# Indicator rows by engine copies, norm weights loaded later, the last row tile in two banks, and half of the first norm rows turned by DMA

## The chip, the cores and the metric

The kernel runs on one core of one Trainium2 chip. The metric is the time of one execution on the device in microseconds (us); lower is better. A core has five engines, each with an instruction stream of its own that it runs in order: TensorE (PE in the profile), VectorE (DVE), ScalarE (ACT), GpSimd (POOL) and SyncE (SP). Weight loads of TensorE have a row of their own (PEld). Engines wait for each other, and for transfers, on semaphores. Transfers are issued from the queues of SP, ACT and POOL; here SP issues nearly all of them, POOL those that change the type on the way (v and the weights).

## The reference

Attention in which each query may look at six chunks of 32 keys, and then a gated feed-forward network (FFN) on the normed result.

```python
# q, k, v: (4, 8, 768, 64)
k_min, k_max = np.min(k_chunks, axis=3), np.max(k_chunks, axis=3)     # 24 chunks of 32 keys
ub = np.sum(np.maximum(q * k_min, q * k_max), axis=-1)                # bound of each chunk
ub = np.where(causal, ub, -1e9)
top_chunks = np.argsort(ub, axis=-1)[..., -6:]
scores = np.matmul(q, k.transpose(0, 1, 3, 2)) / 8
scores = np.where(sel & (pos[:, None] >= pos[None, :]), scores, -1e9)
attn = softmax(scores) @ v
# x: (3072, 512), the attention with its heads side by side
xn = x / np.sqrt(np.mean(x * x, axis=-1, keepdims=True) + 1e-6) * rms_g
g = xn @ w_gate                                                       # 512 -> 1536
out = (g * sigmoid(g) * (xn @ w_val)) @ w_out                         # 1536 -> 512
```

## The kernel before

**A planner writes the order.** The kernel is first built as a list of steps: `add(name, engines, duration, rank, emit, dependencies, opens=..., uses=...)`. `Order.run` then plays the list through with rough durations of its own. Whenever an engine is free it takes, of the steps whose dependencies are done and for whose buffers there is room, the one with the lowest rank; where a step may run on several engines the first free one has it. The instructions are written out in the order in which the steps started. Ranks are sums of constants: `RANK` by kind of step, `TIMES` by place (`a3`: preparation of pair 3, `l3` its loads, `s3.0` its scores, `n0.1` and `f0.1` norm and FFN of batch 0, second half). So a change of one constant can move instructions on all engines. On the chip nothing of that play-through is left but the order: each engine runs its own stream and waits where its operands aren't there yet.

**Attention.** The 32 heads come as 16 pairs (4 per batch). For each pair `prep` loads k and q, turns them on TensorE in threes into PSUM (`pk`, `pq`, L525), evicts them (`kt`, `qt`, L297 on ACT or L301 on DVE), reduces each chunk of 32 keys to its minimum and maximum on DVE (`ku` L556, `kmx` L554, one instruction each for 768 columns) and takes their difference (`dif`, L607, on DVE or POOL). The bounds matmuls (`ub`, L731 for one pair, L789 for two together from pair 6 on) need these and the queries. The bounds are turned back (`up`), masked, and for each query the six best chunks are found on DVE (`MAX8`, L658) and written as a selection (`sel`, L673 to L687), which is turned into rows of the query operand `QS`.

**The indicator rows.** The score matmul (`sc`, L876) contracts over 128 rows: 64 of the head and, beside them, rows that say in `KE` to which chunk a key belongs and in `QS` which chunks a query has chosen; unchosen keys get a large negative score. The rows of `KE` are the same for all pairs: `e_all`, made once on POOL, stands in all three sets of buffers (`SLOTS["set"]` is 3, two heads each). In the kernel before set 0 gets them by two copies on ACT or DVE (`ke0`), sets 1 and 2 by four DMAs on the SP queue (`ke`, L393 and L394).

**Scores to rows.** `exp` on ACT (L893, `pt`), the causal mask on POOL, the product with v on TensorE (`av`, L912), and a division on DVE into `xb`, the rows of a batch.

**Norm and FFN.** `norm` takes three row tiles (half a batch): sums of squares, a root on POOL (`ri`, L981), then on DVE `xs`, the row times its root and the norm weights `gains` (L989). `xs` is turned to `xT`: in batch 0 by four TensorE transposes a row tile (`tp`, L1011) and an eviction, in the other batches by one transposing DMA on SP (L1000). `ffn` then does for 12 blocks of the 1536 columns a `gate` block (4 matmuls, L1045), `tanh` on ACT (`sg`, L1052), `tg` on DVE (L1058), a `val` block (4 matmuls, L1066) and `hh` on DVE (L1074); and for three row tiles 12 matmuls into one PSUM bank (`po`, L1086), an eviction (`osb`, L297 to L303) and a store.

**Fillers.** `busy` (L346) multiplies zeros by zeros: 48 matmuls of 512 columns and 40 of 256 with a rank so high that the planner takes one only where it has nothing else for TensorE. Once written they stand in TensorE's stream and run, whatever the chip's timing.

Of the kernel before, what the change touches and what calls it, by code (L numbers as in the profile page):

```python
# [8 lines left out]
FP32 = mybir.dt.float32  # L9
# [15 lines left out]

RANK = (
    dict(
        av=439.71, dif=-349.0, eps=-276.35, exp=56.9, kC=119.11, kE=221.89, kT=-479.5,
        kload=-91.99, kmn=-561.73, kmx=-221.73, max=-117.69, qC=120.39, qE=644.67, qN=97.14,
        qT=303.27, qX=110.23, qload=17.43, relu=-156.64, root=392.56, sc=392.96, sel=176.91,  # L30
        selC=388.0, selT=-168.59, sq=-325.5, tp=-47.15, tpE=460.17, ub=-387.44, ubE=-1000.64,
        ubm=-238.37, up=-379.03, vload=-360.06, xb=-167.37, xs=293.02,
    ),
    dict(
        av=-243.01, dif=-122.81, eps=-968.41, exp=80.0, gate=-57.45, hh=-33.27, kC=474.21,
        kE=54.78, kT=-28.02, kload=327.35, kmn=571.37, kmx=673.95, mask=-6.85, max=351.72,
        out=-338.93, po=268.25, poE=188.61, qE=-4.14, qN=444.8, qT=271.57, qX=-691.62,
        qload=314.07, relu=202.91, root=-1348.37, sc=-186.72, sel=354.08, sq=285.76, tanh=579.3,
        tg=-259.04, ub=-101.04, ubE=-390.25, ubm=307.49, up=-117.99, val=-52.48, vload=103.56,
        xT=119.23, xb=-299.83, xs=-84.52,  # L40
    ),
)

TIMES = {
# [15 lines left out]
}  # L60


# [139 lines left out]
def kernel(  # L202
# [51 lines left out]
    def add(name, engs, occ, rank, *a, **kw):  # L254
        return order.add(name, engs, occ, rank if isinstance(rank, dict) else {"": rank}, *a, **kw)
# [126 lines left out]
    for n in range(4):  # L382
        prev = add("e_all", "POOL", 0.82, -80 + n, lambda e, n=n: e_step(n), [prev])
    c_e = prev
    c_ke = [None] * NB
    for i in range(NB):
        if i == 0:
            c_ke[i] = add("ke0", "", {"DVE": 1.05, "ACT": 1.4}, {"ke0": 1.0}, lambda e: (
                evict(e, KE[0][0][D:2 * D, :], e_all[:]),
                evict(e, KE[0][1][0:D, :], e_all[:])), [c_e])  # L390
        else:
            c_ke[i] = add("ke", "SP", 1.0, {"ke": 1.0}, lambda e, i=i: (
                nc.sync.dma_start(out=KE[i][0][D:2 * D, :], in_=e_all[:]),  # L393
                nc.sync.dma_start(out=KE[i][1][0:D, :], in_=e_all[:])), [c_e], load=180000)  # L394

    c_kb = []
    if KSIDE < B * NP:
# [89 lines left out]
    def prep(c, i0, nb, at, lr):  # L487
# [8 lines left out]
        for w, src in (("k", k), ("q", q)):  # L496
# [16 lines left out]
            else:  # L513
                ld = [add(w + "load", "SP", 1.4, rank(lr, b, w + "load"), load, opens=[nat[w]],
                          load=n * 550)] * 2
            ready[w] = ld

            evs = []
            for j0 in range(0, nb, 3):
# [425 lines left out]
    def norm(b, half, at, pace):  # L945
# [38 lines left out]
        for j, i in enumerate(rows):  # L984
# [8 lines left out]
            x = add("xs", "DVE", 0.67, rank(at, b, "xs", j, pace), scale, [r, c_gain], opens=[xs],  # L993
                    uses=[XB[b], rt], port=True)

            if b:
                def move(e, i=i, xs=xs):
                    if XT[b].tile is None:
                        tile_of(XT[b], [P, NP, S], BF16, "xT")
                    nc.sync.dma_start_transpose(  # L1000
                        out=XT[b].tile[:, :, i * P:(i + 1) * P], in_=xs.tile[:])

                x = add("xT", "SP", 1.3, rank(at, b, "xT", j, pace), move, [x], opens=[XT[b]],
                        uses=[xs], load=160000)
                XTS[b].setdefault(half, []).append(x)
                continue
# [18 lines left out]
    def ffn(b, c, at, pace):  # L1025
# [10 lines left out]
        for ht in range(NHT):  # L1036
# [38 lines left out]

            hh_done.append(add("hh", "DVE", dve(W), place("hh"), mul, [a, d], opens=[hh], uses=[vp, tg]))
            hhs.append(hh)
        for th in range(3):
            po, ob = Buf("ps", "po"), Buf("ob")
            prev = None  # L1080
            for part in range(3):
                def proj(e, th=th, part=part, po=po):
                    if part == 0:
                        tile_of(po, [P, DM], FP32, "po")
                    for ht in range(part * 4, part * 4 + 4):
                        nc.tensor.matmul(po.tile[:], hhs[ht].tile[:, th * P:(th + 1) * P],  # L1086
                                         wo[:, ht, :], start=(ht == 0), stop=(ht == NHT - 1))

                hs = range(part * 4, part * 4 + 4)
                step()  # L1090
                prev = add("po", "PE", 0.867, place("po"), proj,
                           [prev] + [hh_done[i] for i in hs] + c_wo, opens=[po],
                           uses=[hhs[i] for i in hs])

            def out_(e, po=po, ob=ob):
                t = tile_of(ob, [P, DM], FP32, "osb")
                evict(e, t[:], po.tile[:], 0.5)

            o = add("poE", "", {"ACT": act(512), "DVE": dve(512)}, place("poE"), out_, [prev], opens=[ob], uses=[po])
# [59 lines left out]
```

## Time and profile before

| | us |
|---|---|
| median of 3 runs | 316.25 (315.89 to 316.34) |
| the profiled execution itself | 315.79 |
| its span, first to last instruction | 314.0 |
| TensorE busy | 308.6 |
| DVE busy | 230.7 |
| ACT busy | 194.4 |
| POOL busy | 100.7 |
| granted TensorE clock, mean | 1.00 |

How to read the rows below. The page's first line gives span and instructions, its first part for each engine the busy time, its share and the number of instructions. A row of the waits is "engine instruction <- what it waited for: us in total, times, longest". A row of the groups is line, engine, operation, what it writes and reads, shape and count, then busy us and mean ns of one, then idle time before it. A row of the chain of waits is start, length, engine, tile, line and count; a row of the timeline is start, length, engine, line, operation, tiles, shape, count, and in brackets idle time before it. Both merge equal neighbours. Instructions of an engine overlap by their tails, so the cost of one in a row of equals is the distance of starts, not the length. `SPq`, `ACTq` and `POOLq` rows are issues of DMAs. A row of the DMA view is what is moved, the queue, how often, KB of each and the median us from issue to landing. A row of the windows gives a stretch, its length, then busy us (with counts) of PE, PEld, DVE, ACT and POOL, the clock, the share of the DMA engines and GB/s. `kernel` line numbers are those of the kernel before; in the changed one they are 3 to 7 lower behind the changed places.

### The profile page before, as it was taken

What the parts mean: (1) busy time and instruction counts of PE and PEld (TensorE: products, weight loads), DVE (VectorE), ACT (ScalarE), POOL (GpSimd) and SP (SyncE); (2) the same over time, 40 slices, a digit from 0 to 9 for tenths busy, and PEclk for the clock granted to TensorE, in tenths of its full rate; (3) what the DMA queues carried; (4) which work ended last, traced back from release to release, by engine and by line L of the source; (5) the groups of instructions that cost most, each with busy time, mean ns of one, the idle gap of its engine ahead of it and who ended that gap; (6) DMA issues with size and microseconds to landing.
All of it is one profiled execution on the core that took longest, in us unless ns stands there. A gap on an engine that the chain in (4) does not pass through costs nothing.

```text
span 314.0 us, 7640 instructions
## 1 busy us (share of the span) xinstructions
PE 308.6 (98%) x2844; PEld 196.1 (62%) x2844; DVE 230.7 (73%) x654; ACT 194.4 (62%) x420; POOL 100.7 (32%) x157
## 2 busy tenths in 40 slices
PE   7999999999999999999999999999999999999995
PEld 4567877666566775666667565656666645655542
DVE  7699986888988487967986799879464663873530
ACT  5589987863475987478579654344988823333321
POOL 8666534342353564045357300001522220000000
PEclk9999999999999999999999999999999999999999
DMA  8999989989989898979934640002341045001102
GB/s 171 210 190 178 145 108 207 198 114 143 196 86 199 126 179 152 201 164 222 158 79 61 93 102 0 2 2 52 84 94 59 20 118 150 3 0 65 38 22 111
DMA packets 113301, 35.36 MB, mean 113 GB/s; under 512 B 106224, under 2 KB 110064, under 8 KB 113264
## 3 DMA queue, kind: packets, MB, share of 16 engines
q1 hardware_dynamic: 83152, 26.62, 40.9%
q0 software_dynamic: 28512, 7.87, 25.6%
q10 hardware_dynamic: 1600, 0.39, 0.6%
q8 instruction: 22, 0.36, 0.5%
q14 instruction: 15, 0.12, 0.1%
HBM read 28.57 MB, written 6.29 MB: 111 GB/s over the span
## 4 chain that ended last, share of the span: by engine, by line
PE 97%; DMA 1%; ACTq 0%; ACT 0%; issue 0%
PE gp L1045 20%; PE vp L1066 20%; PE po L1086 20%; PE sc L876 12%; PE av L912 7%; PE busy L346 4%; PE pq L525 4%; PE pk L525 3%; PE ub L789 2%; PE ub L731 2%; DMA qnat<-in_q_dram 1%; PE up L811 1%; PE sc L882 1%; PE up L755 1%; PE tp L1011 0%; ACTq L505 0%
## 5 line engine op out<-in xcount | busy, mean ns | idle before, releaser
L893 ACT ACTIVATE pt<-sc 128x512 bf16<-128x512 f32 (+2 forms) x192 | 88.4, 578 | 10.1 <-PE sc L876 5.3
L1052 ACT ACTIVATE sg<-gp 128x384 bf16<-128x384 f32 x96 | 47.7, 500 | 62.7 <-PE gp L1045 60.0
L1066 PE MATMUL vp<-xT,wv 128*128 128x384 bf16 x384 | 77.0, 326 | 0.0
L1045 PE MATMUL gp<-xT,wg 128*128 128x384 bf16 x384 | 76.2, 326 | 0.0
L1086 PE MATMUL po<-wo,hh 128*128 128x512 bf16 x288 | 69.3, 379 | 0.0
L1058 DVE SCALAR_TENSOR_TENSOR tg<-sg,gp 128x384 bf16<-128x384 bf16 x96 | 52.2, 548 | 21.7 <-ACT sg L1052 19.5
L1074 DVE TENSOR_TENSOR hh<-vp,tg 128x384 bf16<-128x384 f32 x96 | 51.8, 551 | 11.1 <-PE vp L1066 7.3
L1045 PEld LDWEIGHTS <-wg 128*128 128x128 bf16 x384 | 36.8, 98 | 24.5 <-issue 1.0
L1066 PEld LDWEIGHTS <-wv 128*128 128x128 bf16 x384 | 36.9, 98 | 24.1
L876 PE MATMUL sc<-qs,ke 128*128 128x128 bf16 (+5 forms) x420 | 51.4, 251 | 0.0
L1086 PEld LDWEIGHTS <-hh 128*128 128x128 bf16 x288 | 27.6, 98 | 27.5
L301 POOL CAST ke<-kt 64x768 bf16<-64x768 f32 x31 | 26.4, 852 | 36.9 <-ACT kt L297 17.0
L876 PEld LDWEIGHTS <-ke 128*128 128x128 bf16 (+1 forms) x420 | 30.3, 97 | 11.3 <-issue 1.6
L899 POOL TENSOR_SCALAR_AFFINE_SELECT pt<-pt 128x512 bf16<-128x512 bf16 (+1 forms) x48 | 24.4, 527 | 37.6 <-ACT pt L893 37.4
L912 PEld LDWEIGHTS <-pt 128*128 128x128 bf16 x672 | 28.8, 98 | 7.7 <-POOL ke L301 0.6
L912 PE MATMUL av<-vx,pt 128*128 128x65 bf16 x672 | 32.6, 193 | 0.0
L299 ACT ACTIVATE osb<-po 128x512 f32<-128x512 f32 x19 | 11.4, 602 | 21.4 <-PE po L1086 21.4
L346 PE MATMUL busy<-zeros 128*128 128x512 bf16 (+1 forms) x88 | 20.1, 349 | 1.3 <-DVE zeros L341 1.3
L933 DVE TENSOR_TENSOR xb<-av,rden 128x384 bf16<-128x384 f32 (+1 forms) x34 | 18.1, 534 | 1.2
L989 DVE SCALAR_TENSOR_TENSOR xs<-xb,ri,gains 128x512 bf16<-128x512 bf16 x24 | 16.9, 746 | 2.7 <-DMA xT<-xs 2.1
L301 POOL CAST qn<-qnat 128x768 bf16<-128x768 f32 x10 | 8.2, 821 | 31.9 <-DMA qs<-qn 30.7
L481 POOL DMA_DIRECT2D vx<-in_v_dram x16 | 16.8, 1052 | 4.0 <-PE av L912 2.6
(87 smaller groups left out, 303.1 us busy)
## 6 DMA issues: line engine op xcount, KB each, us to landing
out_dram<-osb SPq DMA_DIRECT2D x24, 256.0 KB, 2.2
knat<-in_k_dram SPq DMA_DIRECT2D x30, 192.0 KB, 4.3
qnat<-in_q_dram SPq DMA_DIRECT2D x30, 192.0 KB, 4.8
vx<-in_v_dram POOLq DMA_DIRECT2D x16, 192.0 KB, 4.7
wg<-in_moe_w_gate_dram POOLq DMA_DIRECT2D x2, 768.0 KB, 8.6
wv<-in_moe_w_val_dram POOLq DMA_DIRECT2D x2, 768.0 KB, 7.8
wo<-in_moe_w_out_dram POOLq DMA_DIRECT2D x2, 768.0 KB, 9.9
qs<-qn SPq DMA_TRANSPOSE x26, 3.3
```

The lines of the kernel that those rows point to most:

```text
L301: engine[e].tensor_copy(out_, in_)
L346: nc.tensor.matmul(t[:, 0:n], zeros[:, 0:P], zeros[:, 0:n], start=True, stop=True)
L876: nc.tensor.matmul(t[:, x:x + m, :].rearrange("p a b -> p (a b)"), ke[kk, kb * P:(kb + 1) * P], qs[kk, q0 * P:(q0 + m) * P], start=not tri ...
L893: nc.scalar.activation(out=t[:, 0:nn, :], in_=sc.tile[:, 0:nn, :], func=ACT.Exp, scale=SCALE)
L899: nc.gpsimd.affine_select(out=pt.tile[:, 0:nd, :], in_=pt.tile[:, 0:nd, :], compare_op=ALU.is_ge, fill=0.0, base=0, pattern=[[0, nd], [1, ...
L912: nc.tensor.matmul(av.tile[:, qi - i0, :], pt.tile[:, x, :], VX[c.v.slot][:, hl * NT + kb, :], start=(begin and m == 0), stop=(left[0] == ...
L1045: nc.tensor.matmul(t[:], wg[:, g, hs], XT[b].tile[:, g, cols], start=(g == 0), stop=(g == NP - 1))
L1052: nc.scalar.activation(out=t[:], in_=gp.tile[:], func=ACT.Tanh, scale=0.5)
L1058: nc.vector.scalar_tensor_tensor(out=t[:], in0=sg.tile[:], scalar=1.0, in1=gp.tile[:], op0=ALU.add, op1=ALU.mult)
L1066: nc.tensor.matmul(t[:], wv[:, g, hs], XT[b].tile[:, g, cols], start=(g == 0), stop=(g == NP - 1))
L1074: nc.vector.tensor_tensor(out=t[:], in0=vp.tile[:], in1=tg.tile[:], op=ALU.mult)
L1086: nc.tensor.matmul(po.tile[:], hhs[ht].tile[:, th * P:(th + 1) * P], wo[:, ht, :], start=(ht == 0), stop=(ht == NHT - 1))
```

## The change

Four edits in the code, and all planner constants are new.

- `c_ke`: the rows of all three sets are copied by whichever of DVE, ACT and POOL is free; no DMA is left for them.
- `c_gain` (the load of the norm weights) gets one more dependency: the q load of pair 2.
- The last three row tiles of batch 3, second half: the third one is computed in two PSUM banks of 256 columns each, with an eviction and a store each.
- `norm`: the second half of batch 0 is turned by DMA as well (`if b or half`); its first half stays on TensorE.
- `RANK` and `TIMES`: other values throughout (three lines shown); `FIRST`, `BUSY`, `LATER`, `LIMITS` and `SLOTS` stay as they are.

```diff
-        av=439.71, dif=-349.0, eps=-276.35, exp=56.9, kC=119.11, kE=221.89, kT=-479.5,
+        av=443.28, dif=-47.15, eps=-457.97, exp=190.13, kC=-162.8, kE=103.96, kT=-507.74,
...
-    c_ke = [None] * NB
-    for i in range(NB):
-        if i == 0:
-            c_ke[i] = add("ke0", "", {"DVE": 1.05, "ACT": 1.4}, {"ke0": 1.0}, lambda e: (
-                evict(e, KE[0][0][D:2 * D, :], e_all[:]),
-                evict(e, KE[0][1][0:D, :], e_all[:])), [c_e])
-        else:
-            c_ke[i] = add("ke", "SP", 1.0, {"ke": 1.0}, lambda e, i=i: (
-                nc.sync.dma_start(out=KE[i][0][D:2 * D, :], in_=e_all[:]),
-                nc.sync.dma_start(out=KE[i][1][0:D, :], in_=e_all[:])), [c_e], load=180000)
+    c_ke = [add("ke0", "", {"DVE": 1.05, "ACT": 1.5, "POOL": 1.75}, {f"ke{min(i, 1)}": 1.0}, lambda e, i=i: (
+        evict(e, KE[i][0][D:2 * D, :], e_all[:]), evict(e, KE[i][1][0:D, :], e_all[:])), [c_e], port=True)
+        for i in range(NB)]
...
-            ready[w] = ld
+            ready[w], c.ready = ld, ld[0]
...
-            if b:
+            if b or half:
                 def move(e, i=i, xs=xs):
...
-        for th in range(3):
+        last = b == B - 1 and c == 1
+        for th, c0, cn in [(th, c0, DM >> (last and th == 2)) for th in range(3)
+                           for c0 in ((0, DM // 2) if last and th == 2 else (0,))]:
...
-                        nc.tensor.matmul(po.tile[:], hhs[ht].tile[:, th * P:(th + 1) * P],
-                                         wo[:, ht, :], start=(ht == 0), stop=(ht == NHT - 1))
+                        nc.tensor.matmul(po.tile[:], hhs[ht].tile[:, th * P:(th + 1) * P],
+                                         wo[:, ht, c0:c0 + cn], start=(ht == 0), stop=(ht == NHT - 1))
...
-            add("out", "SP", 0.55, place("out"), lambda e, r0=r0, ob=ob: nc.sync.dma_start(
-                out=out[r0:r0 + P, :], in_=ob.tile[:]), [o], uses=[ob])
+            add("out", "SP", 0.55, place("out"), lambda e, r0=r0, ob=ob, c0=c0, cn=cn: nc.sync.dma_start(
+                out=out[r0:r0 + P, c0:c0 + cn], in_=ob.tile[:]), [o], uses=[ob])
...
         prep(c, 0, NT, f"a{p}", f"l{p}")
+        if p == 2:
+            c_gain.deps.append(c.ready)
```

Where the planner puts things in the changed order, as far as the prediction speaks of it: of the indicator rows, sets 0 and 1 go to ACT and set 2 to DVE. On SP the loads of pair 1 follow those of pair 0 at once, then come the keys of pairs 2 and 3, three pairs' queries, and the loads of a fifth pair; the gains come behind these. TensorE has 87 of the fillers ahead of the first bounds matmuls that follow the first six `gate` blocks, and the last one directly before these. The first FFN half runs six `gate` blocks, then six `val` blocks (in the kernel before they alternate sooner and have scores between them), then the turns of two and a half pairs, then the bounds of three pairs. At the end of the stream the two half banks of the last row tile are done before the three row tiles of batch 3's first half, which come last.

More of the change, by code (lines that the diff above doesn't have):

```diff
@@ L27 @@
     dict(
-        av=439.71, dif=-349.0, eps=-276.35, exp=56.9, kC=119.11, kE=221.89, kT=-479.5,
[L29 to L32, printed above, removed]
+        av=443.28, dif=-47.15, eps=-457.97, exp=190.13, kC=-162.8, kE=103.96, kT=-507.74,
+        kload=18.42, kmn=-811.67, kmx=-125.74, max=-278.17, qC=80.12, qE=884.62, qN=375.44,
+        qT=138.05, qX=513.68, qload=64.94, relu=-468.42, root=250.38, sc=490.04, sel=299.0,
+        selC=351.0, selT=-196.16, sq=-279.88, tp=-231.56, tpE=766.63, ub=-493.06, ubE=-1038.96,
+        ubm=-712.3, up=-442.97, vload=-550.57, xT=-173.0, xb=-257.79, xs=5.81,
     ),
     dict(
[L35 to L40, printed above, removed]
+        av=-444.01, dif=-247.79, eps=-1158.85, exp=-84.07, gate=-107.41, hh=90.47, kC=508.87,
+        kE=121.45, kT=135.04, kload=268.61, kmn=423.77, kmx=1029.28, mask=99.71, max=17.15,
+        out=-545.33, po=509.13, poE=-121.33, qE=47.95, qN=337.07, qT=255.27, qX=-758.65,
+        qload=251.1, relu=311.18, root=-1348.01, sc=-217.1, sel=614.02, sq=331.41, tanh=895.54,
+        tg=59.6, ub=-225.29, ubE=-365.49, ubm=306.15, up=-61.81, val=-66.24, vload=-53.96,
+        xT=338.15, xb=-532.98, xs=-96.07,
     ),
@@ L1081, in ffn, with proj, out_ @@
             for part in range(3):
-                def proj(e, th=th, part=part, po=po):
+                def proj(e, th=th, part=part, po=po, c0=c0, cn=cn):
                     if part == 0:
-                        tile_of(po, [P, DM], FP32, "po")
+                        tile_of(po, [P, cn], FP32, "po")
                     for ht in range(part * 4, part * 4 + 4):
                         nc.tensor.matmul(po.tile[:], hhs[ht].tile[:, th * P:(th + 1) * P],
-                                         wo[:, ht, :], start=(ht == 0), stop=(ht == NHT - 1))
+                                         wo[:, ht, c0:c0 + cn], start=(ht == 0), stop=(ht == NHT - 1))
                 hs = range(part * 4, part * 4 + 4)
                 step()
-                prev = add("po", "PE", 0.867, place("po"), proj,
+                prev = add("po", "PE", 0.867 if cn == DM else 0.44, place("po"), proj,
                            [prev] + [hh_done[i] for i in hs] + c_wo, opens=[po],
                            uses=[hhs[i] for i in hs])
-            def out_(e, po=po, ob=ob):
-                t = tile_of(ob, [P, DM], FP32, "osb")
+            def out_(e, po=po, ob=ob, cn=cn):
+                t = tile_of(ob, [P, cn], FP32, "osb")
                 evict(e, t[:], po.tile[:], 0.5)
-            o = add("poE", "", {"ACT": act(512), "DVE": dve(512)}, place("poE"), out_, [prev], opens=[ob], uses=[po])
+            o = add("poE", "", {"ACT": act(cn), "DVE": dve(cn)}, place("poE"), out_, [prev], opens=[ob], uses=[po])
             r0 = b * S + c * W + th * P
-            add("out", "SP", 0.55, place("out"), lambda e, r0=r0, ob=ob: nc.sync.dma_start(
-                out=out[r0:r0 + P, :], in_=ob.tile[:]), [o], uses=[ob])
+            add("out", "SP", 0.55, place("out"), lambda e, r0=r0, ob=ob, c0=c0, cn=cn: nc.sync.dma_start(
+                out=out[r0:r0 + P, c0:c0 + cn], in_=ob.tile[:]), [o], uses=[ob])
     pairs = []
```

30 rows, old and new, of the table TIMES are left out of this document.

## The prediction

> **What bounds the kernel now.** I read the page first, then TensorE's own waits, then the chain that ended last in order of time, then the other engines at the places that the changed order moves.
>
> ```profile
> span 314.0 us, 7640 instructions
> PE 308.6 (98%) x2844; PEld 196.1 (62%) x2844; DVE 230.7 (73%) x654; ACT 194.4 (62%) x420; POOL 100.7 (32%) x157
> ```
> ```profile
> PE busy L346 <- DVE zeros L341: 1.3, 1, 1.3
> PE pq L525 <- DMA qnat<-in_q_dram: 0.3, 1, 0.3
> ```
> ```profile
> L346 PE MATMUL busy<-zeros 128*128 128x512 bf16 x48 | 13.7, 412 | 1.3 <-DVE zeros L341 1.3
> ```
>
> TensorE is busy for 98% of the span, and its list of waits has two rows: 1.3 us before its first instruction and 0.3 us for the first pair's queries. Busy could hide short gaps, but matmuls also follow each other at their plain distance (the rows of the chain below). So the span is 1.3 us, then one sum over TensorE's instructions, then a tail. In that sum stand 88 `busy` matmuls that compute nothing, the 48 of this row and 40 of half the width. Their order is fixed when the program is built: they run where they stand, needed or not. Hence loads that come sooner save nothing by themselves: the changed kernel also has 48 + 40 fillers, and only fewer or cheaper matmuls or a shorter tail can make it faster. A wait that the order does not cover makes it longer, one for one.
>
> **The change part by part.** The changed planner constants give every engine another order of instructions; what stands where in it is known from the program, and its prices are the distances of starts here:
>
> ```profile
> 7.31 2.37 PE busy L346 x11
> 64.73 0.66 PE pk L525 x6
> 66.69 0.65 PE vp L1066 x4
> 70.10 1.02 PE ub L731 x24
> 85.21 1.45 PE ub L789 x32
> 248.82 12.95 PE po L1086 x60
> ```
> ```profile
> 30.25 0.27 PE L882 MATMUL sc<-trimask,ident_b 128*128 128x256 bf16 x1
> 30.36 0.49 PE L755 MATMUL up<-ident_f,ubs 96*128 96x96 f32 x4
> ...
> 68.48 0.61 PE L1011 MATMUL tp<-ident_b,xs 128*128 128x128 bf16 x8
> 68.92 0.50 PE L525 MATMUL pq<-ident_f,qnat 128*128 128x128 f32 x3
> ```
>
> - Half the first norm rows by DMA: 12 `tp` matmuls go. Eight took 68.92 - 68.48 = 0.44 us, so 0.055 each: -0.66 us of TensorE. It also takes three evictions from ACT or DVE, off the path.
> - Last row tile in two banks: 12 matmuls of 512 columns (12.95 / 60 = 0.216) become 24 of 256 (30.36 - 30.25 = 0.11): 2.64 for 2.59 us, +0.05. The name suggests a shorter tail, but in the changed order three whole tiles of the other half follow the split one; the last eviction and the last store remain of 512 columns. Tail: 0. Were the split tile last, half of the 0.60 us eviction here could go, 0.3 us:
>
> ```profile
> 310.32 0.60 ACT L299 ACTIVATE osb<-po 128x512 f32<-128x512 f32 x1 [0.27 <-PE po L1086]
> ```
>
> - Norm weights loaded later, and no indicator rows by DMA: on the SP queue the gains load and four `ke` copies go from between the first loads.
>
> ```profile
> 3.59 0.34 SPq L437 DMA_DIRECT2D gains<-in_moe_rms_g_dram  x1
> 3.98 1.06 SPq L505 DMA_DIRECT2D knat<-in_k_dram  x2
> ...
> 8.37 0.76 SPq L393 DMA_DIRECT2D ke<-e_all  x1
> ...
> 11.09 1.25 SPq L505 DMA_DIRECT2D knat<-in_k_dram  x2
> ```
> ```profile
> DMA packets 1040, 0.26 MB, mean 241 GB/s; under 512 B 1038, under 2 KB 1038, under 8 KB 1040
> ...
> knat<-in_k_dram SPq DMA_DIRECT2D x2, 192.0 KB, 5.2
> ```
> ```profile
> 7.15 2.54 PE L346 MATMUL busy<-zeros 128*128 128x512 bf16 x11
> ```
>
> The second pair's keys were issued from 3.98 to 5.04 and took 5.2 us to land, so the later head is there at about 9.9. The changed order needs them sooner: at 7.15 it has 8 fillers to go, 8 x 2.37 / 11 = 1.72, so at 8.9. Without the 256 KB of gains ahead (at 241 GB/s, 1.1 us) the keys are there at 8.8. So the wait lies between 0 and 1.0 us (if nothing is gained); I take 0.1. The loads behind it follow 192 KB each 0.8 us, and TensorE asks for them at least as slowly. The gains now go out behind the fifth pair's loads, some 17 us in; their first reader, `xs`, runs at about 50.
>
> The copies that replace the DMAs are two on DVE and two more on ACT at the start:
>
> ```profile
> 0.00:10.00 10.00, 8.41 (x46) 4.16 (x52) 6.64 (x18) 6.02 (x8) 8.14 (x24) 1.00 0.89 183
> ...
> 5.82 1.70 ACT L297 ACTIVATE ke<-e_all 64x768 bf16<-64x768 bf16 x2
> ```
>
> In the first 10 us DVE is busy for 6.64 and ACT for 6.02 (third and fourth number behind the length). About 1.1 us on DVE (estimate, two of the 0.55 us that a copy of 384 columns takes below) and 1.70 on ACT fit, with fillers before TensorE's next real matmul. Behind them queue the evictions `kt` and `qt`; without that cover they would put off TensorE by the same 1.1 to 1.7 us. I take 0.
>
> - The moved order: here I see the largest term. In the changed order TensorE runs six gate blocks of the first FFN half, six value blocks, 21 transposes of new keys and queries, the last filler, the 32 bounds matmuls of two pairs, then 24 of a third. The second twelve of those need `ku` of that third pair (`dif`, L607). From the start of the value blocks TensorE needs 6 x 0.65 + 21 x 0.11 + 0.11 + 1.45 + 0.51 = 8.3 us to that point. DVE, in its order, then still has the rest of one `tg`, two more, three `xs`, six `hh`, and for two pairs the reductions (min and max over 768 columns), one query eviction and `dif`:
>
> ```profile
> 18.27 0.95 DVE L556 TENSOR_REDUCE ku<-kt 128x24 f32<-128x768 f32 x1
> 19.14 0.94 DVE L554 TENSOR_REDUCE kmx<-kt 128x24 f32<-128x768 f32 x1
> ...
> 40.71 0.18 DVE L607 TENSOR_TENSOR ku<-kmx,ku 128x24 f32<-128x24 f32 x1
> ...
> 50.13 2.07 DVE L989 SCALAR_TENSOR_TENSOR xs<-xb,ri,gains 128x512 bf16<-128x512 bf16 x3
> 52.12 0.55 DVE L301 COPY qt<-pq 128x384 f32<-128x384 f32 x1
> ...
> 296.10 0.55 DVE L1058 SCALAR_TENSOR_TENSOR tg<-sg,gp 128x384 bf16<-128x384 bf16 x1 [0.28 <-ACT sg L1052]
> 296.57 0.55 DVE L1074 TENSOR_TENSOR hh<-vp,tg 128x384 bf16<-128x384 f32 x1
> ```
>
> By distances of starts a `tg` or `hh` is 0.47, a reduction 0.87, an `xs` 2.07 / 3 = 0.69, the eviction 0.47, `dif` 0.18: 0.3 + 2 x 0.47 + 3 x 0.69 + 6 x 0.47 + 4 x 0.87 + 0.47 + 0.18 = 10.3. No filler is left there, so TensorE waits 10.3 - 8.3 = 2.0 us. Bounds: 1.4, if DVE stands one `tg` and a signal (0.1) sooner; 2.9, if each of its 18 pieces takes 0.05 more, part of what the full durations have on top. I take 1.9. In the kernel before, the reductions lay singly between FFN blocks. While TensorE waits nothing else of it moves; ScalarE's tanh and the next `hh` come late by as much and keep their distance to it.
>
> - Loads that others now wait for: three transposes of `xT` on SP, and the second halves of the gate and value weights, which go out later on GpSimd's queue, the value half behind the first `wo`.
>
> ```profile
> xT<-xs SPq DMA_TRANSPOSE x6, 2.4
> ...
> wo<-in_moe_w_out_dram POOLq DMA_DIRECT2D x2, 768.0 KB, 9.9
> ...
> qs<-qn SPq DMA_TRANSPOSE x2, 6.5
> ```
>
> A transpose lands after 2.4 us (quiet, 177 to 186 us) to 6.5 (between weight loads, 45 to 50 us). The first gate block that reads the moved ones stands 4.1 us of DVE work and 2.5 us of matmuls behind the last `xs`, 6.6 in all. Wait: 0 to 2.3, if one transpose is queued ahead of the slow one; I take 0. The one query load behind them on SP is wanted some 20 us later. The value half has 12.8 us of matmuls plus the stall between its issue and its reader, some 14 us, for the 9.9 of a weight load: 0, with 4 us of room; the gate half 12.9, likewise.
>
> Sum, against the profiled run's own 315.79 us (span 314.0): -0.66 + 0.05 + 0.1 + 1.9 = +1.4, so 317.2. The three runs have their median 0.46 higher, at 316.25; on that footing 317.6.
>
> **The rivals.**
>
> 1. DVE and GpSimd hold each other up. In the same stretch GpSimd casts two key tiles while DVE runs the two last `xs`.
>
> ```profile
> 24.64 1.82 POOL L301 CAST ke<-kt 64x768 bf16<-64x768 f32 x2 [0.17 <-PE sc L876]
> ...
> 25.70 0.82 DVE L687 TENSOR_SCALAR selq<-m 128x12 bf16<-128x12 f32 x1
> ...
> 33.13 0.19 DVE L687 TENSOR_SCALAR selq<-m 128x12 bf16<-128x12 f32 x1
> ```
>
> The 12-column `selq` took 0.82 us while a cast ran and 0.19 without one; a cast is 0.9. One or two such holds would add 0.8 to 1.7 to the stall: 318.4 to 319.3. Against it: reductions at 18.27 and 19.14 kept their time next to casts. The Trainium skill, "SBUF — State Buffer", section "SBUF: two separate sides", says that the port pair of the two is an exclusive lock, also taken by a DVE operation with two SBUF inputs against a GpSimd operation that reads SBUF. By that rule each `xs` (two such inputs) could lose a whole cast; the `selq` row agrees with a lock.
>
> 2. The other side: TensorE never waits, because DVE is ahead when the value blocks start or its pieces run closer. Then only the 0.6 remains and the time is 315.6. For it speaks that 310 us of wait-free order before show slack everywhere; against it, that this order puts four reductions in one row without a filler behind.
>
> 3. The early loads are late: the keys gain nothing (1.0 more) and the copies on ACT and DVE push evictions, on top of the stall: 318.5.
>
> 4. TensorE's clock falls during the stall.
>
> ```profile
> 1.26 2.74 PE L346 MATMUL busy<-zeros 128*128 128x512 bf16 x6 [1.26 <-DVE zeros L341]
> 3.79 0.85 PE L525 MATMUL pk<-ident_f,knat 128*128 128x128 f32 x3
> ```
>
> At the start six fillers took 3.79 - 1.26 = 2.53 us, 0.42 each, against 0.216 warm: 1.2 us lost. Another such start would give 318.8. The Trainium skill, "TensorE: Matmul & The Clock Gate", section "What's actually happening", puts the fall behind an idle window of about 3.4 us; by that rule a broken 1.9 us would not do it. No row here shows a fall.
>
> **How the numbers follow.** Forecast 0.5, lock 0.17, no wait 0.16, late loads 0.1, clock 0.07. 0.2% of 316.25 is 0.63 us, about what a measurement can tell from no change. The no-wait case lies at -0.6, on that line: about two thirds of it faster, the rest the same; the same also holds a stall half as long. Faster 0.12, same 0.1, slower 0.78. The range runs from the no-wait case, 315.6, to the lock's upper part, 319.1; the likeliest case alone, by its bounds, from 317.1 to 318.6.
>
> **What would show it.** TensorE's waits should have a new row, `ub` for DVE `ku`, of 1 to 2 us in some parts between 65 and 71 us, with the four reductions back to back on DVE; 12 `tp` instead of 24; 24 `po` of 256 columns; a last eviction still of 0.6 us; the second `pk` with no wait, or up to 1 us. The prediction is wrong if no such row stands there, if TensorE waits as long elsewhere (for weights, for `xT`, at the start), or if the last matmul ends before 310 us.

## The result, and the profile after

| | kernel before | changed kernel |
|---|---|---|
| median of the runs (us) | 316.06 (19 runs, 315.46 to 316.42) | 317.25 (19 runs, 316.25 to 318.24) |
| ratio, 95% interval | 1 | 1.0038, 1.0029 to 1.0047 |
| profiled execution: time, span (us) | 315.79, 314.0 | 317.53, 315.8 |

The change costs 1.19 us. The forecast was 317.6 (+1.4). The two profiled executions lie apart by more than the medians: the one of before is 0.27 under its median, the one of the changed kernel 0.28 over its own. So of the 1.8 us between the spans some 1.2 have to be explained, and the runs of the changed kernel also scatter twice as far. The ratios of the runs below leave out executions more than 1.5% above the fastest of the same kernel, so a ratio can stand below the quotient of the medians.

First the head of the page of the changed kernel, then the list of TensorE's waits (us in all, times, longest).

```profile
span 315.8 us, 7631 instructions
PE 307.3 (97%) x2822; PEld 197.0 (62%) x2844; DVE 229.6 (73%) x656; ACT 194.0 (61%) x418; POOL 103.7 (33%) x159
```
```profile
PE busy L346 <- DVE zeros L341: 1.3, 1, 1.3
PE ub L782 <- POOL ku L600: 0.8, 1, 0.8
PE av L905 <- POOL pt L892: 0.6, 1, 0.6
PE sc L869 <- ACT qs L297: 0.5, 1, 0.5
PE ub L724 <- DVE ku L600: 0.3, 1, 0.3
```

TensorE is still the engine that is always busy (2822 of its 2844 records are in the trace), but where before it had two waits it now has five. The row for the first queries is gone, yet that is no gain: the first query transpose starts at the same time in both (first the kernel before, then the changed one).

```profile
5.82 0.52 PE L525 MATMUL pq<-ident_f,qnat 128*128 128x128 f32 x3 [0.34 <-DMA qnat<-in_q_dram]
```
```profile
5.82 0.52 PE L518 MATMUL pq<-ident_f,qnat 128*128 128x128 f32 x3
```

The two `ub` rows are the forecast stall; the `av` and `sc` rows were not forecast. Here is TensorE's timeline around the stall (start, length of the group, and in brackets the idle time in front of it and what ended that).

```profile
60.71 4.06 PE L1059 MATMUL vp<-xT,wv 128*128 128x384 bf16 x24
...
66.90 0.27 PE L346 MATMUL busy<-zeros 128*128 128x256 bf16 x1
67.10 1.12 PE L782 MATMUL ub<-qt,ku 64*32 64x384 f32 x12
...
68.09 0.50 PE L782 MATMUL ub<-rt,ku 64*32 64x384 f32 x4
69.39 0.85 PE L782 MATMUL ub<-rt,ku 64*32 64x384 f32 x8 [0.80 <-POOL ku L600]
69.88 0.78 PE L724 MATMUL ub<-qt,ku 64*32 64x256 f32 x12
70.96 0.65 PE L724 MATMUL ub<-rt,ku 64*32 64x256 f32 x12 [0.30 <-DVE ku L600]
```

From the start of the value blocks to the second twelve it took 70.96 - 60.71 = 10.25 us, where the matmuls alone need 8.3: 1.95 lost. The view of waits shows 1.1 of it, because it counts idle time only from the end of the matmul in front. The last matmuls ahead of the two waits start at 68.11 and 70.29 and run out 0.5 and 0.4 later; by distances of starts the two gaps are 69.39 - 68.11 = 1.28 and 70.96 - 70.29 = 0.67 us, together 1.95. DVE and GpSimd in the same stretch:

```profile
62.45 2.91 DVE L1067 TENSOR_TENSOR hh<-vp,tg 128x384 bf16<-128x384 f32 x6
65.28 1.41 DVE L982 SCALAR_TENSOR_TENSOR xs<-xb,ri,gains 128x512 bf16<-128x512 bf16 x2
66.60 0.95 DVE L549 TENSOR_REDUCE ku<-kt 128x24 f32<-128x768 f32 x1
67.47 0.55 DVE L301 COPY qt<-pq 128x384 f32<-128x384 f32 x1
67.93 0.94 DVE L547 TENSOR_REDUCE kmx<-kt 128x24 f32<-128x768 f32 x1
68.79 0.94 DVE L549 TENSOR_REDUCE ku<-kt 128x24 f32<-128x768 f32 x1
69.65 0.94 DVE L547 TENSOR_REDUCE kmx<-kt 128x24 f32<-128x768 f32 x1
70.63 0.18 DVE L600 TENSOR_TENSOR ku<-kmx,ku 128x24 f32<-128x24 f32 x1
```
```profile
66.07 3.07 POOL L301 CAST ke<-kt 64x768 bf16<-64x768 f32 x3 [6.63 <-ACT kt L297]
69.11 0.23 POOL L600 TENSOR_TENSOR ku<-kmx,ku 128x24 f32<-128x24 f32 x1
```
```profile
66.07 1.30 POOL L301 CAST ke<-kt 64x768 bf16<-64x768 f32 x1 [6.63 <-ACT kt L297]
```

DVE stands without a gap to the subtraction at 70.63, and the last twelve matmuls follow it. The first wait ends with GpSimd's subtraction at 69.11, which stands behind three casts and behind a reduction that DVE ended at 68.87: both were late there. The last row shows the first of the three casts by itself: it started 0.13 us behind the second `xs` on DVE and took 1.30 us, the two behind it 0.82 each.

The `av` row is the other new loss. This is the chain of waits in front of it (start, length, what):

```profile
78.74 1.22 SPq L558
...
80.00 7.91 DMA qs<-qn
...
88.06 1.09 POOL qn L301
89.15 0.77 POOL wo L443
89.92 0.67 POOL pt L892
90.64 0.30 PE av L905 x4
```

Two transposes of chosen queries, issued at 78.74 and 80.00, took 8.3 and 7.9 us, to 87.0 and 87.9. The last of two weight loads (issued at 70.17 and 71.03) was under way until 82.5 and two loads of v behind it until 84.4 and 87.2. GpSimd's next copy into the same buffer waited for them, and in its stream a weight load and the score mask stood behind that copy; TensorE waited for the mask.

Sum of the profiled pair, by distances of starts: -0.6 (matmuls), +1.95 (`ub`), +0.8 (`av`, 0.6 in the list), +0.7 (`sc`, 0.5 in the list) = 2.85, against 1.8 of the spans. So the changed kernel wins about 1.0 elsewhere. Some 0.8 of it are gaps of the kernel before that its list of waits doesn't show, six of less than 0.2 us between 11.8 and 41.5 us. For example, its query transposes at 12.04 start 0.16 later than the four `up` in front of them (11.55) need. They don't stand in the changed order, which has two of its own near 13.7, 0.3 in all. The other 0.5 are not assigned.

### The profile page after: what moved, and what is told of

It is laid out like the page before. It is cut to its first block, busy times and chain, and to the rows that moved or that the text cites. A ratio compares the mean times of both kernels' runs of the same rounds, so it can differ in the third digit from the quotient of the medians.

```text
span 315.8 us, 7631 instructions
## 1 busy us (share of the span) xinstructions
PE 307.3 (97%) x2822; PEld 197.0 (62%) x2844; DVE 229.6 (73%) x656; ACT 194.0 (61%) x418; POOL 103.7 (33%) x159
## 4 chain that ended last, share of the span: by engine, by line
PE 85%; DVE 6%; ACT 3%; DMA 3%; issue 1%; POOL 1%; SPq 0%; POOLq 0%; ACTq 0%; DVEq 0%
PE po L1081 19%; PE vp L1059 16%; PE gp L1038 16%; PE sc L869 11%; PE av L905 6%; PE busy L346 5%; PE pq L518 3%; PE pk L518 3%; DMA qs<-qn 3%; PE ub L782 2%; ACT pt L886 2%; PE ub L724 1%; DVE tg L1051 1%; DVE hh L1067 1%; PE up L804 1%
## 5 line engine op out<-in xcount | busy, mean ns | idle before, releaser
L886 ACT ACTIVATE pt<-sc 128x512 bf16<-128x512 f32 (+2 forms) x192 | 88.9, 591 | 13.4 <-PE sc L869 11.5
L1038 PE MATMUL gp<-xT,wg 128*128 128x384 bf16 x384 | 75.3, 326 | 0.0
L1059 PE MATMUL vp<-xT,wv 128*128 128x384 bf16 x384 | 74.8, 326 | 0.1
L1051 DVE SCALAR_TENSOR_TENSOR tg<-sg,gp 128x384 bf16<-128x384 bf16 x96 | 51.5, 550 | 25.3 <-ACT sg L1045 24.0
L1081 PE MATMUL po<-wo,hh 128*128 128x512 bf16 (+1 forms) x282 | 65.8, 370 | 0.9
L1067 DVE TENSOR_TENSOR hh<-vp,tg 128x384 bf16<-128x384 f32 x96 | 50.9, 552 | 7.9 <-PE vp L1059 4.9
L869 PE MATMUL sc<-qs,ke 89*128 89x128 bf16 (+5 forms) x418 | 53.9, 251 | 0.6 <-ACT qs L297 0.5
L1081 PEld LDWEIGHTS <-hh 128*128 128x128 bf16 x300 | 28.8, 98 | 27.8 <-issue 0.6
L905 PEld LDWEIGHTS <-pt 128*128 128x128 bf16 x672 | 32.4, 98 | 10.2 <-POOL pt L892 1.0
L905 PE MATMUL av<-vx,pt 128*128 128x65 bf16 x672 | 37.5, 194 | 0.6 <-POOL pt L892 0.6
L299 ACT ACTIVATE osb<-po 128x512 f32<-128x512 f32 (+1 forms) x20 | 11.5, 577 | 26.8 <-PE po L1081 26.5
```

The lines of the kernel that those rows point to most:

```text
L869: nc.tensor.matmul(t[:, x:x + m, :].rearrange("p a b -> p (a b)"), ke[kk, kb * P:(kb + 1) * P], qs[kk, q0 * P:(q0 + m) * P], start=not tri ...
L886: nc.scalar.activation(out=t[:, 0:nn, :], in_=sc.tile[:, 0:nn, :], func=ACT.Exp, scale=SCALE)
L905: nc.tensor.matmul(av.tile[:, qi - i0, :], pt.tile[:, x, :], VX[c.v.slot][:, hl * NT + kb, :], start=(begin and m == 0), stop=(left[0] == ...
L1038: nc.tensor.matmul(t[:], wg[:, g, hs], XT[b].tile[:, g, cols], start=(g == 0), stop=(g == NP - 1))
L1051: nc.vector.scalar_tensor_tensor(out=t[:], in0=sg.tile[:], scalar=1.0, in1=gp.tile[:], op0=ALU.add, op1=ALU.mult)
L1059: nc.tensor.matmul(t[:], wv[:, g, hs], XT[b].tile[:, g, cols], start=(g == 0), stop=(g == NP - 1))
```

## The experiments

All kernels but old_consts take the planner's finished list (`done`) and move, drop or replace single steps of it before it is written out, so that everything else keeps its place. Two helpers serve for that:

```python
def step(name, key, i=0): return [s for s in done if s.name == name and key in s.keys][i]
def put(s, before): done.remove(s); done.insert(done.index(before), s)
```

Ratios are to the kernel before, which ran beside each group at 315.91 to 316.00 us.

**gates_first.** Does TensorE wait for DVE's chain, or would it wait anyway?

```diff
+ub = step("ub", "a7")
+put(step("gate", "f0.0", 6), ub); put(step("gate", "f0.0", 7), ub)
+# banks of these two exchanged with those of the two "up" turns
```

> The changed kernel with two gate blocks (the two that stand behind the bounds matmuls) moved ahead of them on TensorE; nothing else moves. Footing: changed kernel 317.25 us, before 316.06. Theory (DVE's chain is late, TensorE waits for it): TensorE does these 1.3 us of matmuls while DVE finishes, the waits ub <- POOL ku (0.8 in the changed kernel) and ub <- DVE ku (0.3) fall to 0.3 or less together, DVE's own instructions keep their times, and the time falls by 0.6 to 1.3 us, to 316.0 to 316.7; not all of it, since DVE is busy 14.5 of the 15 us from 60 to 75 and the next value blocks wait for its tg. Rival A (the second half of the gate weights is what is late; it lands at 66.88): the gate blocks wait in front of the bounds, and the time stays at 317.2 +- 0.3. Rival B (work on DVE is all that counts up to 77 us): every bit of the wait comes back a few us later, again 317.2 +- 0.3, with the wait rows on tg.

Measured: 317.04 us (10 runs), ratio 1.0033 (1.0022 to 1.0044); by time not to be told from the changed kernel, and not the 316.0 to 316.7 of the theory. TensorE's waits in it:

```profile
PE av L905 <- POOL pt L892: 0.7, 1, 0.7
PE gp L1038 <- DMA wg<-in_moe_w_gate_dram: 0.7, 1, 0.7
...
PE vp L1059 <- DVE tg L1051: 0.4, 1, 0.4
```

Both `ub` rows are gone: with 1.3 us of other work in front, DVE and GpSimd are in time, so their late chain was what TensorE waited for. In the trace TensorE comes out of the stretch 0.5 us sooner than in the changed kernel. But both rivals took a share: the gate weights land only then (0.7), and DVE's `tg` is late behind (0.4). The stall was real, and other arrivals stand right behind it.

**relief.** Does a piece taken off DVE come off the wait, one for one?

```diff
+s = step("qE", "a5", 1); s.eng = "ACT"      # behind the last key eviction on ACT
+put(step("dif", "a7"), step("kC", "a5"))
```

> The changed kernel with one eviction of queries (0.47 us by distance of starts) taken from DVE's chain in front of the bounds and given to ScalarE, which has 0.5 us free there, and the small subtraction on GpSimd put ahead of the third key cast, so that the casts don't replace DVE as what comes last. Theory (TensorE waits for the sum of DVE's pieces, one for one): the start of the last twelve bounds matmuls comes 0.45 us sooner against what stands before the stall, and the time falls by 0.45, from 317.25 to 316.8. Rival A (GpSimd's casts are what is late): the subtraction alone gains 0.3, and the time falls by less than 0.3 with no change behind it. Rival B (ScalarE is full): the eviction comes back as a later rt, 317.2 or more.

Measured: 317.79 us (5 runs), ratio 1.0056 (1.0044 to 1.0068).

```profile
PE av L905 <- POOL pt L892: 0.9, 1, 0.9
...
PE ub L724 <- DVE ku L600: 0.5, 1, 0.5
PE ub L782 <- POOL ku L600: 0.2, 1, 0.2
```
```profile
69.87 0.32 DVE L600 TENSOR_TENSOR ku<-kmx,ku 128x24 f32<-128x24 f32 x1
```

In the trace the stretch from the value blocks to the last twelve fell from 10.25 to 9.92 us, 0.33 of the 0.47 taken off. The other 0.14 is in the row above: DVE's subtraction took 0.32 us instead of 0.18, beside a cast on GpSimd that ran until 70.15. The wait `av` grew by 0.25 or so: the slow transposes end at nearly the same time, 87.5 against 87.9 us, whether TensorE comes sooner or not. So the time did not fall, and the forecast of this experiment was wrong in what is behind the stall. That the median is even 0.54 above the changed kernel's is not explained: the profiled execution took 317.19.

**mask_first.** Is the `av` wait the queue behind GpSimd's copy?

```diff
+for s in (step("qN", "a7"), step("qX", "a7")): put(s, step("qX", "a7", 1))   # copy behind the mask
+# step("wo", "w2") put behind both masks
```

> The changed kernel with two score masks on GpSimd's queue moved ahead of the query copy that waits for two slow transposes (it started at 88.06 in the profile, they took 7.9 and 8.3 us), and the second load of the output weights behind them. Theory: the 0.65 us that TensorE waits at 90 us (av <- POOL pt) comes from the mask queueing behind that copy; the row goes and the time falls by 0.65, from 317.25 to 316.6. Rival: the transposes are so late that the scores behind them wait as well, or that wait was in the profiled run only: unchanged, 317.2 +- 0.3.

Measured: 316.77 us (9 runs), ratio 1.0029 (1.0015 to 1.0044). TensorE around the place:

```profile
89.50 0.81 PE L1038 MATMUL gp<-xT,wg 128*128 128x384 bf16 x4
90.16 0.29 PE L905 MATMUL av<-vx,pt 128*128 128x65 bf16 x4
```

The wait is gone: from the gate block to `av` it is 0.66 us, the block's own length, against 90.64 - 89.17 = 1.47 in the changed kernel, though the transposes there still took 7.0 and 7.3 us. The median is 0.48 lower, less than these 0.8; the intervals overlap, so the trace, not the time, carries this.

**tail_last.** The prediction said that splitting the row tile helps only where the split tile is last.

```diff
+last = sorted((s for s in done if "f3.1" in s.keys), key=lambda s: s.n)[-5:]   # its three po, eviction, store
+done = [s for s in done if s not in last] + last
```

> The changed kernel with the second half of the split row tile put last on TensorE, ScalarE and SP; the three whole tiles that followed it now precede it. Theory (the prediction's: the split shortens the tail only where the split tile is last): last eviction of 256 columns 0.38 us instead of 0.60, last store 128 KB with 1.7 us to landing instead of 2.1: -0.2 to -0.6 us, 316.65 to 317.05, and 4.0 us or less from the last matmul's start to the end of the span instead of 4.17. Rival: the tail is a fixed latency of the store, whatever it carries: no more than the eviction's -0.2.

Measured: 316.80 us (12 runs), ratio 1.0029 (1.0018 to 1.0040): 0.45 below the changed kernel, with intervals that overlap. The last eviction of the changed kernel, of tail_last and of gains_tail (below):

```profile
312.10 0.60 ACT L299 ACTIVATE osb<-po 128x512 f32<-128x512 f32 x1 [1.13 <-PE po L1081]
```
```profile
312.19 0.38 ACT L299 ACTIVATE osb<-po 128x256 f32<-128x256 f32 x1 [0.76 <-PE po L1081]
```
```profile
310.26 0.38 ACT L299 ACTIVATE osb<-po 128x256 f32<-128x256 f32 x1 [0.93 <-PE po L1090]
```

The spans end 3.7 us behind that start in the changed kernel (and before: 314.0 - 310.32), 3.2 in tail_last, 3.1 in gains_tail. Of the 0.5, 0.22 is the eviction; the rest goes with the smaller store (128 KB land in 1.7 us, 256 KB in 2.1, in the changed kernel's list of DMA issues). From the start of the last matmul to the end of the span it is 4.2 us in the changed kernel, 3.6 in tail_last and 3.5 in gains_tail.

**no_half_fillers.** Are the fillers only ballast?

```diff
+fill = [s for s in done if s.name == "busy"][BUSY:]
+done = [s for s in done if s not in fill]
```

> The changed kernel without its 40 half-width fillers (they compute nothing that is read). Theory 1 (fillers are a fixed cost in the sum, needed or not): 40 x 0.11 = 4.4 us less, 312.9. Theory 2 (each stands where TensorE would have waited for ScalarE's exponentials and DVE's norm anyway): the same places now show waits, av <- ACT pt and tp <- DVE xs between 43 and 54 us, 3.9 us or more in all, and the time falls by 0 to 0.5 only, 316.75 to 317.25. Theory 3 (fillers keep the clock of TensorE up): the granted clock falls behind these gaps and the time rises by 0.5 or more.

Measured: 319.10 us (5 runs), ratio 1.0098 (1.0083 to 1.0112): 4.4 us of matmuls taken out, and 1.85 us slower than the changed kernel. The windows of it (stretch, length, busy us and count of PE, PEld, DVE, ACT, POOL, then the granted clock of TensorE, DMA share, GB/s):

```profile
45.00:47.70 2.70, 2.70 (x45) 2.12 (x43) 2.63 (x7) 2.70 (x7) 1.24 (x2) 1.00 1.13 127
47.70:50.30 2.60, 1.02 (x12) 0.50 (x11) 2.34 (x7) 2.55 (x8) 2.03 (x4) 1.00 1.36 224
50.30:57.20 6.90, 6.72 (x61) 5.57 (x63) 4.94 (x12) 4.83 (x12) 2.98 (x5) 0.51 1.18 215
57.20:60.00 2.80, 2.74 (x35) 1.93 (x35) 1.23 (x4) 2.77 (x7) 2.57 (x5) 1.00 0.52 92
```

For 2.6 us TensorE has work in thin slices only, between ScalarE's exponentials. Then its clock is 0.51 for 6.9 us, which loses 6.9 x 0.49 = 3.4 us. Theory 1 falls. The waits of theory 2 are there (`av` for ACT's `pt`, 1.6 in all): at 50.4 us this kernel and the changed one stand level, so up to there the waits cost what the fillers did. From there to 56.4 it falls 1.6 us behind, in the stretch with the low clock, and stays so to the end: theory 3. So in this profile the fillers are worth their time because they hold the clock. The five runs are not alike, though: their mean clocks go from 0.988 to 0.998, and the run with 0.998 took 318.21.

**transpose_only, transpose_banks.** The first edit alone, in the order of the kernel before, in place of the 12 `tp`; then with two banks exchanged.

```diff
 def turn(e, xs=xs, tp=tp, i=i):
+    if half:      # and its eviction left out
+        nc.sync.dma_start_transpose(out=XT[b].tile[:, :, i * P:(i + 1) * P], in_=xs.tile[:])
+        return
```

> The kernel before, in its own order, with one of the change's edits alone: the three xT tiles of the second half of the first batch turned by DMA in the place where 12 tp matmuls and three evictions stood. Footing: before 316.06 us. Theory (prediction's term, 12 x 0.055): -0.66, 315.4. Rival A (a bank): the bounds matmuls right behind need a bank that DVE's tg frees at a time that does not move, so TensorE waits there for what the tp matmuls took: a new row ub <- DVE tg of about 0.6 and a time of 315.9 to 316.1. Rival B (transposes beside weight loads land after 6 us): the first gate block of that half waits for xT, and the time is 316.5 or more.

> As transpose_only, with two PSUM banks exchanged for the steps from these bounds to the value block behind (the bounds take a bank that the tp matmuls no longer use). Theory: now the whole 0.66 shows, 315.4, and no row ub <- DVE tg. If the bank was not what TensorE waited for: as transpose_only.

Measured: 317.64 us (12 runs, 316.03 to 321.74), ratio 1.0053 (1.0027 to 1.0080); with the banks 317.76 (6 runs), 1.0062 (1.0038 to 1.0086). Waits of transpose_only, and its slowest transpose in the chain:

```profile
PE gp L1053 <- DMA xT<-xs: 2.2, 1, 2.2
...
PE ub L731 <- DVE tg L1066: 0.5, 1, 0.5
```
```profile
63.48 9.76 DMA xT<-xs
```

Both rivals are true at once. The bank row (0.5) goes when the banks are exchanged. The large cost is the transposes: three issued from 60.6 to 63.5, right behind a value-weight load of 60.26, took 9.5 to 10.5 us and landed at 71.1 to 73.3, the load itself at 70.84. Plain loads fare alike: a key load of 192 KB issued at 50.23, behind the gate weights of 49.57, took 10.2 us, against a median of 4.1 for the key loads of this run. In before and in the changed kernel the transposes of `xT` later on, without such loads, take 2.4 to 2.5 us in the median.

**wv_earlier.** The same with that load issued ten microseconds sooner.

```diff
+done.insert(done.index(step("wg", "w1")) + 1, done.pop(done.index(step("wv", "w1"))))
```

> transpose_banks (before's order, xT of the second half by DMA) with the load of the second half of the value weights issued right behind that of the gate weights, some 10 us sooner. Theory (a transposing DMA issued while a weight load is under way lands only with or behind that load; in transpose_only xT landed at 71.09 and 71.52, the load at 70.84): the load now lands at 64 to 67, the three xT land within 1 us of it or by themselves in about 2.5 us, by 68; the wait gp <- DMA xT goes, and the time is 315.2 to 315.7, with the small spread of the kernel before. Rival (such transposes are slow there whatever loads stand ahead of them): they take 8 us or more, the wait stays, 316.5 or more.

Measured: 319.85 us (12 runs; one at 315.07, the others 318.68 to 321.11), ratio 1.0075 (1.0044 to 1.0105). SP's queue, and two windows:

```profile
52.78 8.27 SPq L505 DMA_DIRECT2D qnat<-in_q_dram  x2
61.10 3.76 SPq L505 DMA_DIRECT2D knat<-in_k_dram  x2
64.96 5.37 SPq L1012 DMA_TRANSPOSE xT<-xs  x3
```
```profile
70.60:73.50 2.90, 0.14 (x6) 0.00 (x0) 0.42 (x1) 0.86 (x2) 2.33 (x3) 1.00 1.59 137
73.50:74.50 1.00, 0.95 (x6) 0.61 (x7) 0.00 (x0) 0.10 (x1) 0.00 (x0) 1.00 0.94 146
74.50:78.00 3.50, 3.50 (x16) 2.06 (x14) 2.04 (x4) 0.39 (x1) 0.00 (x0) 0.51 1.44 184
```

The transposes did get faster (4.3 to 5.7 us, no weight load ahead), but SP's issues of the key and query loads in front of them now took up to 8.27 us for two, so the transposes went out 3.9 us later (64.96 against 61.08 in transpose_banks). TensorE waited 2.8 us for them, and in the profiled execution that wait cost it the clock as well (0.51 for 3.5 us). Two runs with a mean clock of 1.00 took 318.68 and 318.98, so most of the loss is there without it. My theory covered the landing, not the issue.

**gains_later, combined, gains_tail.** The later norm weights alone; then with the transposes and a split last tile; then without the transposes.

```diff
+put(step("gains", ""), step("kload", "l4"))
 # in ffn, for the very last tile (combined and gains_tail): 24 matmuls into two banks at its end
+for y, c0 in ((po, 0), (po2, DM // 2)):
+    for ht in range(NHT):
+        nc.tensor.matmul(y.tile[:], hhs[ht].tile[:, th * P:(th + 1) * P], wo[:, ht, c0:c0 + DM // 2], ...)
```

> The kernel before with the load of the norm weights moved on SP's queue behind the loads of the first four pairs; nothing else. Theory (the prediction: earlier loads save nothing by themselves where fillers stand): 0 to -0.3 us (the 0.3 if the first queries land sooner), 315.75 to 316.06. Rival: the 256 KB ahead of the second pair's keys is what sets the start: -1.0, 315.0.

> The kernel before in its own order with transpose_banks, gains_later and its last row tile computed in two halves of 256 columns, each evicted and stored by itself, at the very end. Theory: -0.66 (12 tp matmuls), 0 to -0.3 (loads), +0.05 (24 half matmuls for 12), -0.2 to -0.6 (tail): 314.6 to 315.25, faster than both kernels. Rival (the terms share one cause or the tail is fixed): 315.4 or more.

> The kernel before with gains_later and its last row tile in two halves of 256 columns at the very end (combined without the xT transposes). Theory (the terms add: gains_later gave 315.55 against 315.91; the tail gives -0.2 to -0.5 and +0.05): 315.1 to 315.4, faster than both kernels. Rival (the tail is a fixed latency): 315.5 to 315.7.

Measured: gains_later 315.55 us (11 runs), ratio 0.9991 (0.9982 to 1.0000); combined 317.14 (12 runs, up to 320.83), 1.0039 (1.0015 to 1.0063), with the row `gp <- DMA xT` again; gains_tail 315.00 (6 runs, 314.87 to 315.52), 0.9973 (0.9961 to 0.9984). The last beats both kernels, by 0.3% over the one before; in its profile nearly all of that is the shorter tail. gains_later and gains_tail lie 0.1 to 0.2 under their forecasts, combined 1.9 over its own. It differs from gains_tail by the transposes and the exchanged banks alone: the transposes are what spoilt it.

**old_consts.** All four edits with the constants of before.

```diff
-RANK, TIMES of the changed kernel
+RANK, TIMES of before, "ke1" for "ke", xT.0 = 119.23
```

> The changed kernel's code with the planner constants of before (two keys that they lack take the value of the nearest one: ke1 that of ke, xT.0 that of xT.1). Theory 1 (the prediction: the edits give -0.6 and the new constants' order costs 1.9): 315.4 or so. Theory 2 (constants fit only the program for which they were found; other steps shift the whole order, and transposes and loads meet in other places): new waits of some us on DMA, 318 to 322.

Measured: 326.43 us (4 runs, 322.68 to 327.96), ratio 1.0292 (1.0248 to 1.0336). Theory 2, and more than it said. The constants of before do not bring back the order of before: with the other code the planner makes a third order of them, and two of its keys were filled in. Its largest wait:

```profile
PE gp L1038 <- DMA xT<-xs: 7.3, 2, 5.3
```

Here too the three transposes of the second half went out right behind a value-weight load (from 62.66, the load at 62.26), and took 9.5 to 11.7 us.

## Why the prediction was right, and where not

- **What bounds the kernel.** Right: TensorE's instructions one after another, plus waits. The sentence that fillers run "needed or not" is true of the order, but as an argument that fewer matmuls are the way to a faster kernel it is incomplete: without 40 of them the clock falls. And the sum is not free of gaps: 0.8 us of short ones lay in the kernel before, under what its list of waits shows.
- **12 tp matmuls, -0.66; two banks, +0.05; tail 0.** The counts are in the trace, and the last eviction is still 0.60 us. "Were the split tile last" was put at 0.3; it is 0.5 from the start of the last eviction, since the smaller store also lands sooner.
- **Early loads and copies, 0.1.** The second pair's keys started at 8.88 without a wait, as worked out. That nothing is gained by earlier loads was too hard: gains_later is 0.36 us below its kernel before, at the edge of what can be told, and in its profile 0.34 is won between 11.5 and 21 us, most of it in two gaps of the kernel before (at 12.0 and 19.7) that no filler covered. The first queries give nothing (5.82 us in both kernels). The term also varies: in runs whose order up to there is that of the changed kernel, the first bounds matmuls start up to 0.66 later than in it (mask_first) and 0.17 sooner (relief).
- **The moved order, 1.9.** Place and size held: 1.95, with DVE last behind four reductions and one query eviction. gates_first and relief show the cause. The sum left out GpSimd: the larger of the two waits ends with its subtraction, behind three casts, and with that put ahead of the third cast (relief) the row falls from 0.8 to 0.2. What the step also did not see is that this wait is not the last barrier: the gate weights, the `tg` and the slow query transposes stand so close behind that moving work into the stall gave 0.5 us in the trace and 0.2 by the medians, which can't be told from nothing.
- **xT by DMA, 0.** Right in the changed order, where the one transpose beside a weight load took 6.0 us and had room. Wrong as a property of the edit: in the order of before it costs 1.7 us net, the saved matmuls included. The upper bound of 6.5 was the median of two transposes, 7.0 and 6.0, behind a weight load that took only 7.5 us: they landed 0.7 and 1.5 us behind it. In transpose_only the load took 10.6, and the transposes landed 0.3 to 2.4 behind it, after 9.5 to 10.5. So what has to be priced is when the load in front lands. The new constants are then not only a cost of 1.9, as I had them: they put the value weights behind the transposes (load at 71.03, last `xT` issued at 67.3). In the two other orders that were run the transposes stand behind that load.
- **Not in the sum.** The `av` wait, 0.8 by distances of starts: I costed the transposes of `xT` for SP's queue and weight loads and left out those of the queries, which meet weight and v loads at 79 us, with the mask queued behind them on GpSimd. mask_first shows this path. The `sc` wait, 0.7 so counted, was not tested. So 1.5 us of losses were missing from the sum, and about 1.0 of gains, half of it from the short gaps of the kernel before. They nearly cancel, and that the total came out 0.4 under the spans' difference and 0.2 over that of the medians (+1.19) is luck to that extent; the place and the size of the stall are not.
- **The rivals.** DVE lost nothing in the stall of the changed kernel: its two `xs` took 1.41 us there, 0.70 each, the plain distance. GpSimd did: the cast that started 0.13 us behind an `xs` took 1.30 us instead of 0.82, and without these 0.48 the three casts would have ended at some 68.7 (an estimate), ahead of DVE's reduction at 68.87. In relief the subtraction of DVE came second and took 0.32 instead of 0.18, until the cast was over. Both agree with the rule of the Trainium skill, "SBUF — State Buffer", section "SBUF: two separate sides", by which the one that starts first has the port pair for its whole instruction. So the rival's mechanism was there, with the other loser and at most 0.5 us. No late start. No fall of the clock in this stall, where TensorE was busy for about two thirds of the three worst microseconds.

Open: whether mask_first, tail_last and a removed stall together bring the changed kernel below the one before was not tried.

## What to carry to other kernels

Price a DMA by what was issued just ahead of it, in its landing and in its issue, and follow what stands in the same stream behind its reader. When a wait is found, ask for the next arrival behind it before counting the wait as a gain. An edit and the order around it have to be judged as one: here the transposes by DMA are harmless in one order and cost 1.7 us in the other.

## What was not expected of the hardware

TensorE's clock halved after less than I thought: after 2.6 us in which it still had 12 thin matmuls (no_half_fillers), and 1.0 us after the end of one wait of 2.8 us (wv_earlier); it stayed at 0.51 for 6.9 and 3.5 us, although TensorE was busy all that time. The Trainium skill, "TensorE: Matmul & The Clock Gate", section "What's actually happening", asks for an idle window of about 3.4 us; these runs fell in less, and the first was not idle throughout, so here the measurements decide. A transposing DMA issued right behind a 768 KB load took 9.5 to 10.5 us (transpose_only) for what takes 2.4 in the median without one, and landed only when that load had.
